# First products of the second stage with 128 rows, one chunk at a time

## The chip, the cores and the metric

One core of one Trainium2 chip runs the whole program. The metric is the device time of one execution in microseconds (us). The engines are TensorE (PE; its loads of weights are listed apart as PEld), VectorE (DVE), ScalarE (ACT), GpSimd (POOL) and SyncE (SP), which issues the transfers.

## What is computed

Windowed attention gives 2304 tokens of 512 numbers. A mixture of experts with 32 slots follows, and then a dense layer with 2048 hidden units, which is where the change lies. The reference, cut to these two:

```
def _moe_ref(x, phi, w1, w2):
    logits = x @ phi                              # 2304 x 32
    d = softmax of logits over the tokens
    slot_input = (d.T @ x).reshape(8, 4, 512)
    for e in range(8):
        slot_out[e] = np.maximum(slot_input[e] @ w1[e], 0.0) @ w2[e]
    c = softmax of logits over the slots
    return c @ slot_out                           # 2304 x 512

def _moe2_ref(x, w_in, w_out):
    h = x @ w_in                                  # 2304 x 2048
    g = h - np.tanh(h)
    return g @ w_out
```

Since the dense layer's input is `c @ slot_out`, its first product is `c @ (slot_out @ w_in)`: with `G = slot_out @ w_in` (32 x 2048) each hidden value needs a sum over 32 slots only.

## The kernel before, in words

The program runs through attention, the dispatch to the experts, the experts (`sop`, line 920), and from about 180 us the second stage, the function `second`. That stage treats the 2048 hidden units in 16 chunks `f` of 128, and the 18 blocks of 128 tokens in groups: A (blocks 0 to 3), EG (16 and 17), BG (4 to 7), C and DG (four blocks each). Its phases are, in order: A and EG with chunks 0 to 7, whose sums are put aside; BG with all 16 chunks; A and EG with chunks 8 to 15; C; DG.

For each batch of up to three chunks a projection comes first: `p` (line 1057) multiplies `slot_out` with four quarters of `w_in` into the four groups of 32 rows, `g` (line 1061) is its copy by ACT, and line 1065 multiplies that by the 128x128 matrix `dev` (in the tile `more`), which sums the four quarters and leaves the result in all four groups of 32 rows. ACT casts it to the tile `Gs` (line 1073); line 1067 makes `GT`, from which DVE gets the coefficients `co` (lines 1080 to 1083). `cT` holds the combine weights `c`, with tokens as columns, as four groups of 32 rows: high part, low part, high part, low part. A sum over 64 rows, high and low, is therefore the whole product.

A first product `h` (line 1191) takes a chunk's 128 columns of `Gs` as weights and streams the columns of `cT` of a group of tokens, 512 or, for EG, 256. `Gs` holds even chunks in rows 0 to 63 and odd ones in rows 64 to 127, and two chunks' products are issued one after the other, each on its own half of the rows by `tile_position`. Only the products of chunks 0 and 1 in the first phase are issued alone, each behind two products (line 1188) whose result is overwritten. From each `h` ACT makes `u` (line 1199), DVE makes `r` (line 1206), or for some chunks ACT makes `d` (line 1210) and POOL `r` (line 1214). Then, for each block of tokens, PE adds `r` times `wh`, the chunk of `w_out`, into `acc` (line 1163); one further product per block takes `cT` and `Ms`. `msum` and `mrep` make `Ms`. Weights come as 64-bit words in pieces `raw_i` and `raw_o`, from which POOL and ACT make halves (lines 348 to 353) that DVE merges (line 358). A later second load of all pieces (line 974, lines 979 and 981), `kmax`, `marks` and `verdict` check the ranges.

The order of all this is written by a planner, the class `Plan`: it is given each operation's engine, duration, inputs and buffers, lists the operations greedily by priority, tries 500 changes of the priorities, keeps the list with the least estimated end, and emits it. Each engine then works strictly in that order. Buffers that matter here: four PSUM tiles for `h` (shared with `p` and a few others), four for `acc`, three `u`, five `r`.

Of the kernel before, what the change touches and what calls it, by code (L numbers as in the profile page):

```python
# [11 lines left out]
F32R = mybir.dt.float32r  # L12
# [13 lines left out]
DM, NS, E, FE, FF = 512, 32, 8, 1024, 2048  # L26
# [57 lines left out]
class Plan:  # L84
# [4 lines left out]
    def add(self, *alts, deps=(), take=(), free=(), ready=0.0, boost=0.0):  # L89
        t = dict(alts=alts, deps=[d for d in deps if d is not None], take=take, free=free, ready=ready, boost=boost, id=len(self.tasks))  # L90
        self.tasks.append(t)
        for tag, key in take:
            if tag in self.ordered:
                self.ordered[tag].append(key)
        return t
# [178 lines left out]
def attention_moe_moe(ctx: ExitStack, tc: tile.TileContext, q, k, v, phi, w1, w2, w_in, w_out, cst, out, dbg=None):  # L274
    nc = tc.nc
# [680 lines left out]
    def second(raw, cT, store, more, wh0):  # L956
# [28 lines left out]
        DMA_AT = -0.5  # L985
        dev, devT, big = more[:, 0:128], more[:, 128:161], more[:, 161:].bitcast(F16)
        nc.vector.tensor_scalar(out=dev, in0=sel4, scalar1=sel4[:, NS - 1:NS], scalar2=0.125, op0=ALU.subtract, op1=ALU.mult)
        nc.vector.tensor_scalar(out=devT[:, 0:NS], in0=sel, scalar1=sel[:, NS - 1:NS], scalar2=5.0, op0=ALU.subtract, op1=ALU.mult)
        nc.gpsimd.memset(devT[:, NS:], 1.0 / NS)
        nc.gpsimd.memset(big, 2.0 ** 13)  # L990
        for f in range(NF // 2):
            nc.gpsimd.tensor_scalar(out=wh0[:, f, :], in0=place(("o", f)), scalar1=8.0, scalar2=0.0, op0=ALU.mult, op1=ALU.add)
        res, el, ps = yield
        Gs = res.tile([128, FF // 2], F32R, name="Gs")
        wh1 = res.tile([128, NF // 2, DM], F32R, name="wh1")
        whi = lambda f: (wh0 if f < NF // 2 else wh1)[:, f % (NF // 2), :]
        GT = res.tile([128, NF, NS + 1], F32, name="GT")
# [6 lines left out]
        live = {}  # L1004
        plan = Plan(dict(raw=RAW, h=4, acc=4, u=3, r=5, d=2, g1=2, o=8, code=2))
        add = plan.add

        def one(eng, dur, emit):
            return [(eng, dur, emit)]

        P = {}
# [3 lines left out]
        for k, piece in enumerate(PRE + loads):  # L1015
            kind, f = piece
# [27 lines left out]
            b = next(b for b in batches if f in b)  # L1044
            if f != b[-1]:
                continue
            n, f0 = len(b), b[0]
            tag = "acc" if f0 < 2 else "h"
            key = (tag, f0 if f0 < 2 else ("p", f0))
            def mk(b=b, n=n, f0=f0, tag=tag):  # L1050
# [15 lines left out]
                    for x in range(n):  # L1066
                        nc.tensor.matmul(t[:, 128 * n + 33 * x:128 * n + 33 * (x + 1)], lhsT=g1[:, 128 * x:128 * (x + 1)], rhs=devT, start=True, stop=True)

                def gs(y):
                    first = f0 + (f0 % 2 != y)  # L1070
                    m = len([x for x in b if x % 2 == y])
                    src = live["p", f0][64 * y:64 * y + 64, 0:128 * n].rearrange("p (n x) -> p n x", n=n)[:, first - f0::2]
                    nc.scalar.copy(Gs[64 * y:64 * y + 64, 128 * (first // 2):128 * (first // 2 + m)].rearrange("p (n x) -> p n x", n=m), src)

                def gt_copy():
                    nc.scalar.copy(GT[:, f0:f0 + n, :], live["p", f0][:, 128 * n:161 * n].rearrange("p (n x) -> p n x", n=n))
# [9 lines left out]
            fa, fg, fb, fh, ft, fc = mk()  # L1086
            lead = 8.0 - 2.0 * f0 if f0 < 2 else 0.0
# [2 lines left out]
                P["A", x] = a  # L1090
            g = add(one("ACT", 0.15 + 0.11 * n, fg), deps=[a], take=[("g1", f0)], boost=lead)
            bb = add(one("PE", 0.1 + 0.35 * n, fb), deps=[g], free=[("g1", f0)], boost=lead)
            for y in range(2):
                m = len([x for x in b if x % 2 == y])
                if m:
                    gh = add(one("ACT", 0.15 + 0.11 * m, lambda fh=fh, y=y: fh(y)), deps=[bb], free=[key], boost=lead)
                    for x in b:
                        if x % 2 == y:
                            P["G", x] = gh
            gc = add(one("ACT", 0.25, ft), deps=[bb], free=[key], boost=lead)  # L1100
            joint = next(y for y in joints if f0 in y)
            if f == joint[-1]:
# [31 lines left out]
        m = add(one("PE", 3.8, m_sum), deps=[P["pt", f] for f in range(NF)] + [P["mg", ("o", f)] for f in range(NF)], take=[("h", "m")])  # L1134
        m = add(one("ACT", 0.49, lambda: nc.scalar.activation(out=M4s, in_=live["m"], func=AF.Copy, scale=-2.0 / 15.0)), deps=[m], free=[("h", "m")])
        m = add(one("PE", 0.95, m_rep), deps=[m], take=[("h", "mr")])
        m = add(one("ACT", 0.49, lambda: nc.scalar.copy(Ms, live["mr"])), deps=[m], free=[("h", "mr")])
# [13 lines left out]
        for tiles, fs, aff, into in phases:  # L1151
# [20 lines left out]
            if aff == "first":  # L1172
                for t in tiles:
                    affine(t, phase_no)
            twos = [[f] for f in (0, 1)] if phase_no == 0 else []
            twos += [[f, f + 1] for f in fs if f % 2 == 0 and (phase_no or f > 1)]
            for two in twos:
                sub = tiles
                w, c0 = 128 * len(sub), 128 * sub[0]
                size = w / 512  # L1180
                idle = 2 if len(two) == 1 else 0
                name = lambda f, p=phase_no, t=tiles[0]: (p, f, t)

                def hid(two=two, w=w, c0=c0, name=name, idle=idle):
                    for f in two:
                        live["h", name(f)] = ps.tile([128, 512], F32, tag="h", name=f"h_{name(f)[0]}_{f}_{c0}", bufs=4)[:, 0:w]
                    for _ in range(idle):
                        nc.tensor.matmul(live["h", name(two[0])], lhsT=cT[:, 0:128], rhs=cT[:, c0:c0 + w], start=True, stop=True)
                    for f in two:
                        y = 64 * (f % 2)  # L1190
                        nc.tensor.matmul(live["h", name(f)], lhsT=Gs[y:y + 64, 128 * (f // 2):128 * (f // 2 + 1)], rhs=cT[y:y + 64, c0:c0 + w], start=True, stop=True, tile_position=(y, 0))  # L1191

                prev_h = h = add(one("PE", 0.03 + 0.23 * size + 0.35 * idle, hid), deps=[P["G", f] for f in two] + [prev_h], take=[("h", name(f)) for f in two])
                for f in two:
                    key = name(f)

# [348 lines left out]
```

## Time and profile before

| | |
|---|---|
| three runs | 299.88, 302.53, 305.98 us; median 302.53 |
| profiled execution | 302.16 us |
| its span | 300.3 us |
| busy, share of the span | PE 95%, DVE 67%, POOL 54%, ACT 50% |
| mean granted TensorE clock | 0.995 of full speed |
| `h` products (line 1191) | 80, 19.1 us busy |
| output products (`acc`, line 1163, without `Ms`) | 288, 80.3 us busy |

The span is from the first to the last instruction; the device time holds 1.9 us more around it. Matmuls are pipelined: a record's duration overlaps those of its neighbours, so the price of a product is read from the starts. A row of the timeline merges consecutive instructions of a kind: start, length, engine, line, what, how many.

### The profile page before, as it was taken

The numbers are of one execution on the slowest core, as the hardware profiler recorded it, in microseconds if no ns is written. First come the engines' busy times: TensorE is split into PE (matmuls) and PEld (weight loads), VectorE is DVE, ScalarE is ACT, GpSimd is POOL, SyncE is SP. The second block draws the span as 40 slices with busy tenths as digits, with TensorE's granted clock in tenths as the row PEclk, the third lists the DMA queues.
The fourth block names the chain that finished last, engine by engine and source line by source line (L and its number), as shares of the span: only waits on it lengthen the run. The fifth ranks groups of instructions, "written<-read, shape, count | busy, mean of one in ns | idle before, by whom it ended". The sixth has DMA issues, their size and how long they took to land.

```text
span 300.3 us, 7499 instructions
## 1 busy us (share of the span) xinstructions
PE 285.3 (95%) x2684; PEld 187.0 (62%) x2684; DVE 202.1 (67%) x693; ACT 151.4 (50%) x290; POOL 162.0 (54%) x240
## 2 busy tenths in 40 slices
PE   5999999999999999989999879999999999999991
PEld 3778888878788887653334215565665666576660
DVE  5559999688799897515323109889962768638972
ACT  2266655635374455421222018678863747757741
POOL 8639867865877660010516019981573657676320
PEclk9999999999999999999999999999999999999997
DMA  7989999879797889999999999952989999703004
GB/s 200 246 248 356 283 321 364 285 247 308 236 359 226 309 286 386 410 408 406 410 404 410 410 392 395 411 193 76 313 293 363 314 375 339 310 0 106 36 0 150
DMA packets 62699, 86.95 MB, mean 290 GB/s; under 512 B 19008, under 2 KB 48064, under 8 KB 62656
## 3 DMA queue, kind: packets, MB, share of 16 engines
q1 hardware_dynamic: 61568, 86.15, 82.4%
q8 instruction: 23, 0.38, 0.5%
q10 hardware_dynamic: 1088, 0.26, 0.4%
q14 instruction: 20, 0.16, 0.2%
HBM read 81.67 MB, written 4.72 MB: 288 GB/s over the span
## 4 chain that ended last, share of the span: by engine, by line
PE 78%; DMA 11%; DVE 5%; ACT 2%; issue 1%; SPq 0%; DVEq 0%; ACTq 0%
PE acc L1163 26%; PE sc L544 10%; PE pv L574 7%; PE pp L563 6%; PE h L1191 5%; DMA X<-in_moe_w 3%; DMA w<-in_moe_w 3%; DMA store<-in_moe_w 3%; PE tr_q L472 3%; PE xt L489 3%; PE tr_k L472 3%; PE sop L920 2%; PE lp L505 2%; PE hp L901 2%; PE sp L808 2%; PE warm L684 1%
## 5 line engine op out<-in xcount | busy, mean ns | idle before, releaser
L1163 PE MATMUL acc<-wh,r 128*128 128x512 f32 x288 | 80.3, 410 | 0.4 <-DVE r L1206 0.4
L1163 PEld LDWEIGHTS acc<-wh,r 128*128 128x128 f32 x288 | 50.7, 188 | 19.1 <-issue 7.0
L1199 ACT ACTIVATE u<-h,co 128x512 f32<-128x512 f32 (+1 forms) x80 | 48.8, 646 | 24.1 <-PE h L1191 17.1
L1206 DVE SCALAR_TENSOR_TENSOR r<-h,co,u 128x512 fp32r<-128x512 f32 (+1 forms) x66 | 43.8, 689 | 12.9 <-PE acc L1163 6.9
L548 DVE CUSTOM_DVE_ANT_0 sm<-sc,m_sb 128x96 f32<-128x96 f32 x144 | 29.2, 257 | 9.0 <-PE sc L544 9.0
L544 PE MATMUL sc<-kT,qT 64*64 64x96 f32 (+1 forms) x608 | 34.4, 253 | 0.3 <-ACT kT L465 0.3
L564 ACT ACTIVATE pT<-pp 96x512 f32<-96x512 f32 x38 | 23.1, 608 | 16.9 <-PE pp L563 16.9
L544 PEld LDWEIGHTS sc<-kT,qT 64*64 64x64 f32 x608 | 27.0, 134 | 5.0 <-issue 1.7
L1214 POOL TENSOR_TENSOR r<-d,u 128x512 fp32r<-128x512 f32 (+1 forms) x14 | 18.6, 1328 | 19.6 <-ACT d L1210 8.7
L439 POOL TENSOR_SCALAR vw<-vw 32x256 f32<-32x256 f32 (+1 forms) x40 | 24.9, 623 | 4.0 <-DMA vw<-in_v 1.1
L574 PE MATMUL pv<-vw,pT 97*64 97x65 f32 x608 | 26.1, 227 | 0.1
L482 ACT COPY qT<-tr_q 128x512 f32<-128x512 f32 x16 | 13.7, 858 | 24.6 <-PE tr_q L472 24.6
L574 PEld LDWEIGHTS pv<-vw,pT 97*64 97x64 f32 x608 | 20.8, 137 | 7.7 <-issue 6.5
L552 DVE TENSOR_TENSOR sm<-sm,mx 128x384 f32<-128x384 f32 (+1 forms) x38 | 24.7, 650 | 1.2
L563 PE MATMUL pp<-c_sb,sm 128*96 128x128 f32 x152 | 23.5, 277 | 0.1
L498 ACT COPY xT<-xt 128x512 f32<-128x512 f32 (+1 forms) x19 | 14.1, 767 | 11.0 <-PE xt L489 10.4
L1191 PE MATMUL h<-cT,Gs 64*128 64x512 f32 (+1 forms) x80 | 19.1, 468 | 0.0
L353 POOL TENSOR_SCALAR pre<-raw_o 128x512 bf16<-128x512 int16 x16 | 13.8, 870 | 9.3 <-DMA raw_o<-in_moe_w_out 8.9
L563 PEld LDWEIGHTS pp<-c_sb,sm 128*96 128x96 f32 x152 | 16.2, 126 | 3.2 <-issue 1.4
L606 DVE TENSOR_TENSOR X<-pv,rd 128x256 f32<-128x256 f32 (+3 forms) x52 | 16.5, 340 | 1.0
L901 PE MATMUL hp<-w,store 128*32 128x512 f32 x120 | 16.0, 596 | 1.2 <-DVE store L1386 1.2
L1191 PEld LDWEIGHTS h<-cT,Gs 64*128 64x128 f32 x80 | 7.5, 183 | 14.4 <-issue 9.8
(218 smaller groups left out, 479.0 us busy)
## 6 DMA issues: line engine op xcount, KB each, us to landing
w<-in_moe_w SPq DMA_DIRECT2D x54, 512.0 KB, 10.1
raw_i<-in_moe_w_in SPq DMA_DIRECT2D x32, 512.0 KB, 7.1
raw_o<-in_moe_w_out SPq DMA_DIRECT2D x32, 512.0 KB, 6.6
q<-in_q SPq DMA_DIRECT2D x16, 256.0 KB, 4.4
k<-in_k SPq DMA_DIRECT2D x16, 256.0 KB, 4.4
X<-in_moe_w SPq DMA_DIRECT2D x8, 512.0 KB, 9.4
out<-X SPq DMA_DIRECT2D x14, 256.0 KB, 3.8
vw<-in_v SPq DMA_DIRECT2D x16, 144.0 KB, 4.7
```

The source lines that it names most:

```text
L439: copy = lambda dst, src: nc.gpsimd.tensor_scalar(out=dst, in0=src, scalar1=1.0, scalar2=0.0, op0=ALU.mult, op1=ALU.add)
L544: nc.tensor.matmul(dst[half, lo:hi], lhsT=qT[u % NQ][half, i:i + QB], rhs=keys[half], start=True, stop=True)
L548: nc.vector.tensor_tensor_reduce(out=sm[:, o:o + n, :].rearrange("p g k -> p (g k)"), in0=sc[:, o:o + n, :].rearrange("p g k -> p (g k)"), ...
L552: nc.vector.tensor_tensor(out=sm[:, o:o + n], in0=sm[:, o:o + n], in1=mx[:, o:o + n].unsqueeze(2).to_broadcast([128, n, KB]), op=ALU.subtract)
L563: nc.tensor.transpose(pp[:, i, :], sm[:, i, :], ident)
L564: nc.scalar.activation(out=pT[0:KB], in_=pp, func=AF.Exp, scale=0.125)
L574: nc.tensor.matmul(pv[64 * ab:64 * ab + 64, i, :], lhsT=pT[:, o + x, 64 * ab:64 * ab + 64], rhs=w[:, ab, u % 2, j + x, :], start=x == 0, s ...
L901: nc.tensor.matmul(hp[32 * dc:32 * dc + 32, :], lhsT=siTs[e % 2][:, dc, :], rhs=w_of(f"1{e}", dc)[:, 512 * hf:512 * (hf + 1)], start=e % 2 ...
L1163: nc.tensor.matmul(live[key], lhsT=lhsT(), rhs=rhs(), start=new, stop=n == due)
L1191: nc.tensor.matmul(live["h", name(f)], lhsT=Gs[y:y + 64, 128 * (f // 2):128 * (f // 2 + 1)], rhs=cT[y:y + 64, c0:c0 + w], start=True, stop ...
L1199: nc.scalar.activation(out=live["u", key], in_=live["h", key], func=AF.Square, scale=co[:, SC, f:f + 1])
L1206: nc.vector.scalar_tensor_tensor(out=live["r", key], in0=live["h", key], scalar=co[:, BB, f:f + 1], in1=live["u", key], op0=ALU.add, op1=A ...
```

## The change

`Gs` gets a column range for every chunk (2048 columns instead of 1024). The right half of `dev` is set to zero by POOL, so that line 1065's product has zeros in rows 64 to 127; the cast to `Gs` takes all 128 rows and all chunks of a batch in one instruction. An `h` is one product over 128 rows, without a tile position: the first 64 rows give the sum over high and low part, the other 64 add zero. Each `h` is an operation of its own for the planner, with a new duration (0.004 + 0.228 for 512 columns, in place of 0.03 + 0.23 for a pair).

```diff
--- before.py
+++ after.py
@@ -985,13 +985,14 @@
         DMA_AT = -0.5
         dev, devT, big = more[:, 0:128], more[:, 128:161], more[:, 161:].bitcast(F16)
         nc.vector.tensor_scalar(out=dev, in0=sel4, scalar1=sel4[:, NS - 1:NS], scalar2=0.125, op0=ALU.subtract, op1=ALU.mult)
+        nc.gpsimd.memset(dev[:, 64:], 0.0)
         nc.vector.tensor_scalar(out=devT[:, 0:NS], in0=sel, scalar1=sel[:, NS - 1:NS], scalar2=5.0, op0=ALU.subtract, op1=ALU.mult)
         nc.gpsimd.memset(devT[:, NS:], 1.0 / NS)
         nc.gpsimd.memset(big, 2.0 ** 13)
         for f in range(NF // 2):
             nc.gpsimd.tensor_scalar(out=wh0[:, f, :], in0=place(("o", f)), scalar1=8.0, scalar2=0.0, op0=ALU.mult, op1=ALU.add)
         res, el, ps = yield
-        Gs = res.tile([128, FF // 2], F32R, name="Gs")
+        Gs = res.tile([128, FF], F32R, name="Gs")
         wh1 = res.tile([128, NF // 2, DM], F32R, name="wh1")
         whi = lambda f: (wh0 if f < NF // 2 else wh1)[:, f % (NF // 2), :]
         GT = res.tile([128, NF, NS + 1], F32, name="GT")
@@ -1066,11 +1067,8 @@
                     for x in range(n):
                         nc.tensor.matmul(t[:, 128 * n + 33 * x:128 * n + 33 * (x + 1)], lhsT=g1[:, 128 * x:128 * (x + 1)], rhs=devT, start=True, stop=True)
 
-                def gs(y):
-                    first = f0 + (f0 % 2 != y)
-                    m = len([x for x in b if x % 2 == y])
-                    src = live["p", f0][64 * y:64 * y + 64, 0:128 * n].rearrange("p (n x) -> p n x", n=n)[:, first - f0::2]
-                    nc.scalar.copy(Gs[64 * y:64 * y + 64, 128 * (first // 2):128 * (first // 2 + m)].rearrange("p (n x) -> p n x", n=m), src)
+                def gs():
+                    nc.scalar.copy(Gs[:, 128 * f0:128 * (f0 + n)], live["p", f0][:, 0:128 * n])
 
                 def gt_copy():
                     nc.scalar.copy(GT[:, f0:f0 + n, :], live["p", f0][:, 128 * n:161 * n].rearrange("p (n x) -> p n x", n=n))
@@ -1090,13 +1088,9 @@
                 P["A", x] = a
             g = add(one("ACT", 0.15 + 0.11 * n, fg), deps=[a], take=[("g1", f0)], boost=lead)
             bb = add(one("PE", 0.1 + 0.35 * n, fb), deps=[g], free=[("g1", f0)], boost=lead)
-            for y in range(2):
-                m = len([x for x in b if x % 2 == y])
-                if m:
-                    gh = add(one("ACT", 0.15 + 0.11 * m, lambda fh=fh, y=y: fh(y)), deps=[bb], free=[key], boost=lead)
-                    for x in b:
-                        if x % 2 == y:
-                            P["G", x] = gh
+            gh = add(one("ACT", 0.15 + 0.11 * n, fh), deps=[bb], free=[key], boost=lead)
+            for x in b:
+                P["G", x] = gh
             gc = add(one("ACT", 0.25, ft), deps=[bb], free=[key], boost=lead)
             joint = next(y for y in joints if f0 in y)
             if f == joint[-1]:
@@ -1172,13 +1166,11 @@
             if aff == "first":
                 for t in tiles:
                     affine(t, phase_no)
-            twos = [[f] for f in (0, 1)] if phase_no == 0 else []
-            twos += [[f, f + 1] for f in fs if f % 2 == 0 and (phase_no or f > 1)]
-            for two in twos:
+            for two in [[f] for f in fs]:
                 sub = tiles
                 w, c0 = 128 * len(sub), 128 * sub[0]
                 size = w / 512
-                idle = 2 if len(two) == 1 else 0
+                idle = 2 if phase_no == 0 and two[0] < 2 else 0
                 name = lambda f, p=phase_no, t=tiles[0]: (p, f, t)
 
                 def hid(two=two, w=w, c0=c0, name=name, idle=idle):
@@ -1187,10 +1179,9 @@
                     for _ in range(idle):
                         nc.tensor.matmul(live["h", name(two[0])], lhsT=cT[:, 0:128], rhs=cT[:, c0:c0 + w], start=True, stop=True)
                     for f in two:
-                        y = 64 * (f % 2)
-                        nc.tensor.matmul(live["h", name(f)], lhsT=Gs[y:y + 64, 128 * (f // 2):128 * (f // 2 + 1)], rhs=cT[y:y + 64, c0:c0 + w], start=True, stop=True, tile_position=(y, 0))
-
-                prev_h = h = add(one("PE", 0.03 + 0.23 * size + 0.35 * idle, hid), deps=[P["G", f] for f in two] + [prev_h], take=[("h", name(f)) for f in two])
+                        nc.tensor.matmul(live["h", name(f)], lhsT=Gs[:, 128 * f:128 * (f + 1)], rhs=cT[:, c0:c0 + w], start=True, stop=True)
+
+                prev_h = h = add(one("PE", 0.004 + 0.228 * size + 0.35 * idle, hid), deps=[P["G", f] for f in two] + [prev_h], take=[("h", name(f)) for f in two])
                 for f in two:
                     key = name(f)
```

Names in the following rows: `h_0_1024` is chunk 0 for the tokens from 1024 on; `r_10_16` is chunk 10 for the group that begins with block 16; the last number of a name counts tiles.

PE, the passage from phase EG with chunks 8 to 15 to phase C, before:

```order
L1191 MATMUL h_0_1024_3588<-cT,Gs 128x512
L1191 MATMUL h_1_1024_3589<-cT,Gs 128x512
L1163 MATMUL acc_17_3568<-wh_2793,r_11_16_3566 128x512
L1163 MATMUL acc_17_3568<-wh_2793,r_12_16_3575 128x512
L1163 MATMUL acc_16_3557<-wh_2793,r_12_16_3575 128x512
L1163 MATMUL acc_16_3557<-wh_2793,r_13_16_3586 128x512
L1163 MATMUL acc_17_3568<-wh_2793,r_13_16_3586 128x512
L1163 MATMUL acc_2_3448<-Ms,cT 128x512
L1163 MATMUL acc_16_3557<-wh_2793,r_14_16_3601 128x512
L1163 MATMUL acc_17_3568<-wh_2793,r_14_16_3601 128x512
L1191 MATMUL h_2_1024_3616<-cT,Gs 128x512
L1191 MATMUL h_3_1024_3617<-cT,Gs 128x512
```

and now:

```order
L1182 MATMUL h_0_1024_3602<-cT,Gs 128x512
L1182 MATMUL h_1_1024_3608<-cT,Gs 128x512
L1157 MATMUL acc_16_3573<-wh_2794,r_10_16_3551 128x512
L1182 MATMUL h_2_1024_3613<-cT,Gs 128x512
L1157 MATMUL acc_17_3580<-wh_2794,r_11_16_3583 128x512
L1157 MATMUL acc_16_3573<-wh_2794,r_12_16_3590 128x512
L1157 MATMUL acc_17_3580<-wh_2794,r_12_16_3590 128x512
L1157 MATMUL acc_16_3573<-wh_2794,r_15_16_3617 128x512
L1182 MATMUL h_3_1024_3627<-cT,Gs 128x512
L1157 MATMUL acc_16_3573<-wh_2794,r_13_16_3598 128x512
L1182 MATMUL h_4_1024_3632<-cT,Gs 128x512
```

The products `h`, which stood in pairs with eight output products between them, are spread: five of them now stand in the place of four, one, five and one output products apart.

DVE at the start of the second stage, from the first `r` to the second, before (`co` is of chunks 2 to 4, line 358 merges a weight piece, `raw_i_2708` being a later one than `raw_i_2704`):

```order
L1206 SCALAR_TENSOR_TENSOR r_0_0_2891<-h_0_0_2853,co,u_0_0_2882 128x512
L358 SCALAR_TENSOR_TENSOR X_76<-raw_i_2704,X_76 128x512
L1080 TENSOR_SCALAR co<-GT 128x3
L1081 TENSOR_TENSOR co<-co 128x3
L1082 TENSOR_SCALAR co<-co 128x3
L1083 SCALAR_TENSOR_TENSOR co<-co 128x3
L358 SCALAR_TENSOR_TENSOR X_76<-raw_i_2708,X_76 128x512
L1206 SCALAR_TENSOR_TENSOR r_1_0_2928<-h_1_0_2867,co,u_1_0_2910 128x512
```

and now:

```order
L1197 SCALAR_TENSOR_TENSOR r_0_0_2884<-h_0_0_2857,co,u_0_0_2875 128x512
L1078 TENSOR_SCALAR co<-GT 128x3
L1079 TENSOR_TENSOR co<-co 128x3
L1080 TENSOR_SCALAR co<-co 128x3
L1081 SCALAR_TENSOR_TENSOR co<-co 128x3
L358 SCALAR_TENSOR_TENSOR X_76<-raw_i_2704,X_76 128x512
L1197 SCALAR_TENSOR_TENSOR r_1_0_2910<-h_1_0_2879,co,u_1_0_2900 128x512
```

The merge of `raw_i_2708` has moved behind the second `r`; the merge of `raw_o_2700`, which stood ahead of the first coefficients, has moved to a place far behind.

PE at the same place, from the second half of the projection of chunk 1 on, before (`h_0_0_2853<-cT` are the products that are overwritten, `p_2820` is the projection of chunks 2 to 4, `p_2843` of 5 to 7):

```order
L1067 MATMUL p_2813<-more,g_1_2831 128x33
L1057 MATMUL p_2843<-pre,phi_sb 32x384 x4
L1188 MATMUL h_0_0_2853<-cT 128x512 x2
L1191 MATMUL h_0_0_2853<-cT,Gs 128x512
L1188 MATMUL h_1_0_2867<-cT 128x512 x2
L1191 MATMUL h_1_0_2867<-cT,Gs 128x512
L1065 MATMUL p_2820<-g_2_2858,more 128x384
L1067 MATMUL p_2820<-more,g_2_2858 128x33 x3
L1065 MATMUL p_2843<-g_5_2865,more 128x384
L1067 MATMUL p_2843<-more,g_5_2865 128x33 x3
L1163 MATMUL acc_0_2897<-wh_2692,r_0_0_2891 128x512
```

and now:

```order
L1068 MATMUL p_2814<-more,g_1_2832 128x33
L1058 MATMUL p_2844<-pre,phi_sb 32x384 x4
L1180 MATMUL h_0_0_2857<-cT 128x512 x2
L1182 MATMUL h_0_0_2857<-cT,Gs 128x512
L1066 MATMUL p_2821<-g_2_2862,more 128x384
L1068 MATMUL p_2821<-more,g_2_2862 128x33 x3
L1180 MATMUL h_1_0_2879<-cT 128x512 x2
L1182 MATMUL h_1_0_2879<-cT,Gs 128x512
L1066 MATMUL p_2844<-g_5_2869,more 128x384
L1068 MATMUL p_2844<-more,g_5_2869 128x33 x3
L1182 MATMUL h_2_0_2902<-cT,Gs 128x512
```

A half of a projection now stands between the first two `h`, and a third `h` ahead of the first output product; the projection of chunks 8 to 10 (`p_2914` before) has moved from the first phase to the change from the second to the third.

POOL, where the second stage's constants are set, before (`more` holds `dev`, in its first 128 columns, and two smaller constants; `wh_2692` is `wh0`):

```order
L922 MEMSET store 128x8x4 x2
L922 MEMSET X_76 128x8x4 x2
L989 MEMSET more 128x1
L990 MEMSET more 128x32
L992 TENSOR_SCALAR wh_2692<-pre 128x512 x8
L353 TENSOR_SCALAR X_76<-raw_i_2696 128x512
```

and now:

```order
L922 MEMSET store 128x8x4 x2
L922 MEMSET X_76 128x8x4 x2
L988 MEMSET more 128x64
L990 MEMSET more 128x1
L991 MEMSET more 128x32
L993 TENSOR_SCALAR wh_2692<-pre 128x512 x8
L353 TENSOR_SCALAR X_76<-raw_i_2696 128x512
```

The memset of the right half of `dev` stands ahead of the two small ones and the eight copies of `wh0`.

## Rows read from the trace of the kernel before

**Rows 1.** Chain that ended last, 192.7 to 294 us: shares by line.
```profile
by line: PE acc L1163 75.7%; PE h L1191 14.8%; PE msum L1128 3.5%; PE p L1057 1.3%; PE p L1065 1.1%; PE p L1067 0.9%; PE mrep L1132 0.8%; DVE okt L1318 0.5%; DVE okt L1317 0.4%; PE marks L1341 0.3%; PE kmax L1274 0.2%; issue 0.2%; DVE okt L
```

**Rows 2.** Windows: us; busy of PE, PEld, DVE, ACT, POOL; clock; DMA share; GB/s.
```profile
180.00:205.00 25.00, 24.41 (x138) 14.54 (x130) 22.52 (x54) 18.63 (x43) 20.77 (x29) 1.00 0.80 303
192.70:206.70 14.00, 13.99 (x58) 8.61 (x58) 12.47 (x31) 9.82 (x20) 8.86 (x16) 1.00 0.52 187
206.70:224.70 18.00, 18.00 (x89) 11.48 (x89) 14.74 (x25) 14.07 (x28) 9.88 (x19) 1.00 0.78 264
224.70:294.00 69.30, 69.30 (x300) 43.93 (x299) 47.24 (x96) 42.23 (x73) 37.56 (x42) 1.00 0.59 207
```

**Rows 3.** Chain that ended last, 179.5 to 193 us, in order of time.
```profile
182.90 1.20 DVE pre L358
...
189.62 0.69 DVE X L358
```

**Rows 4.** PE in order of time, 264.5 to 290 us.
```profile
267.16 0.51 PE L1191 MATMUL h<-cT,Gs 64*128 64x512 f32 x2
267.60 3.91 PE L1163 MATMUL acc<-wh,r 128*128 128x512 f32 x16
271.43 0.50 PE L1191 MATMUL h<-cT,Gs 64*128 64x512 f32 x2
271.87 0.73 PE L1163 MATMUL acc<-wh,r 128*128 128x512 f32 x2
272.53 0.51 PE L1191 MATMUL h<-cT,Gs 64*128 64x512 f32 x2
```

**Rows 5.** PE in order of time, 196.4 to 203.5 us.
```profile
198.47 0.38 PE L1191 MATMUL h<-cT,Gs 64*128 64x256 f32 x2
198.78 1.18 PE L1163 MATMUL acc<-wh,r 128*128 128x512 f32 x4
199.89 0.38 PE L1191 MATMUL h<-cT,Gs 64*128 64x256 f32 x2
```

**Rows 6.** PE in order of time, 205 to 225 us.
```profile
206.78 0.85 PE L1057 MATMUL p<-X,phi_sb 128*32 128x384 f32 x8
207.57 0.73 PE L1163 MATMUL acc<-wh,r 128*128 128x512 f32 x2
...
209.69 0.81 PE L1065 MATMUL p<-g,more 128*128 128x384 f32 x2
210.34 0.75 PE L1067 MATMUL p<-more,g 128*128 128x33 f32 x6
210.92 2.35 PE L1163 MATMUL acc<-wh,r 128*128 128x512 f32 x9
213.20 0.73 PE L1191 MATMUL h<-cT,Gs 64*128 64x512 f32 x4
213.86 2.37 PE L1163 MATMUL acc<-wh,r 128*128 128x512 f32 x9
```

**Rows 7.** PE's groups by shape, 192.7 to 294 us.
```profile
L1191 PE MATMUL h<-cT,Gs 64*128 64x512 f32 x60 | 14.5, 490 | 0.0
...
L1191 PE MATMUL h<-cT,Gs 64*128 64x256 f32 x16 | 3.1, 381 | 0.0
```

**Rows 8.** PE in order of time, 273.4 to 277 us.
```profile
276.32 0.39 PE L1163 MATMUL acc<-Ms,cT 128*128 128x512 f32 x1
276.56 0.63 PE L1163 MATMUL acc<-wh,r 128*128 128x512 f32 x2
```

**Rows 9.** POOL in order of time, 150 to 180 us.
```profile
157.80 5.42 POOL L992 TENSOR_SCALAR wh<-pre 128x512 fp32r<-128x512 f32 x8
178.47 0.77 POOL L353 TENSOR_SCALAR X<-raw_i 128x512 bf16<-128x512 int16 x1 [15.25 <-DMA raw_i<-in_moe_w_in]
```

**Rows 10.** DVE in order of time, 160 to 171 us.
```profile
164.31 0.28 DVE L987 TENSOR_SCALAR more<-c_sb 128x128 f32<-128x128 f32 x1
```

**Rows 11.** Instructions on the tile h: duration ns min/median/max, first and last start.
```profile
L1199 ACT ACTIVATE u<-h,co x80: 467/688/712, 185.0 to 288.3; 128x512 f32<-128x512 f32 x64, 128x256 f32<-128x256 f32 x16
L1206 DVE SCALAR_TENSOR_TENSOR r<-h,co,u x66: 469/743/753, 186.7 to 289.6; 128x512 fp32r<-128x512 f32 x52, 128x256 fp32r<-128x256 f32 x14
```

## Prediction

> **What bounds the kernel now.** I read the chain that ended last first. From 192.7 us to the verdict near 294 us it runs on TensorE alone: 75.7% of that stretch are the output products (line 1163), 14.8% are the first products `h` (line 1191) that the change rewrites, some 15 us [rows 1]. The windows agree: PE is busy in every microsecond of the three stretches behind 192.7, at a granted clock of 1.00, while DVE and ACT have room, but little of it at first: DVE works 12.47 of 14.0 us, then 14.74 of 18.0, then 47.24 of 69.3 [rows 2]. So behind 192.7 a microsecond less on PE is a microsecond less of the kernel, as long as the other engines follow. Before 192.7 it is not: there the chain runs through DVE, over merges of the weights, coefficients and the first `r` [rows 3]. The end (verdict, flag, last store) hangs on the last PE products and moves with them; both programs have four output products behind the verdict.
>
> **What a visit to `h` costs on PE.** I take starts, since ends are modelled. Two visits with 16 output products between them start 4.27 us apart, two with 2 between them 1.10 us [rows 4]: 14 products make 3.17 us, 0.23 each, and 1.10 - 2 x 0.23 leaves 0.64 for the visit, a pair of 512 columns. Other such gaps give 0.62 to 0.64; I use 0.63. The two of a pair run side by side, or they could not be back within 0.44 us [rows 4]; a block of two pairs is back after 0.66, so the second pair adds about 0.23 and the block costs 0.86 [rows 6]. So 0.23 of a visit is streaming, and about 0.40 is paid for going to 64-row tiles and back. A pair of 256 columns: 1.42 us from one visit to the next with 4 products between [rows 5] leaves 0.50, its neighbours 0.51 and 0.53; I use 0.515.
>
> **What it will cost.** The new `h` is a product with 128 rows, 128 columns of weights and 512 or 256 streamed columns. The trace holds it under another name: `acc<-Ms,cT` has the same shape and type with `cT` as one operand, stands among output products, and the next starts 0.23 us later [rows 8]. I price an `h` of 512 columns at 0.23. One of 256 is not in the trace. Below it cannot be under the six 33-column records, 0.58 us together, 0.10 each [rows 6]; above, not over the 0.23 of 512. I take 0.12, half of 0.23, nearer to the lower end, because 0.10 at 33 columns shows that the exchange of weights does not hold it longer. Sixteen of them: 1.9, between 1.6 and 3.7.
>
> **The sum on the path.** Behind 192.7 stand 60 `h` of 512 columns and 16 of 256 [rows 7]: 26 single pairs and two blocks of four, and eight pairs of 256. Of the 26, 24 lie between output products: 24 x (0.63 - 0.46) = 4.1. Two follow work of another kind whose own change of kind stays, so I give them half, 0.2. The blocks of four lose: 2 x (0.86 - 0.92) = -0.1. The narrow pairs: 8 x (0.515 - 0.24) = 2.2. Together 6.3 us; with 256 columns at 0.23 it would be 4.5, at 0.10 6.7. Of the 6.3, the visits before 224.7 (five pairs, one behind the projection, both blocks of four, four narrow pairs) hold 1.9, the rest 4.4.
>
> **What moves, and what that costs.** The planner gets new durations, so all engines are re-ordered from chunk 0 on. At the start, DVE does two merges less before the third `r`, worth 1.20 + 0.69 us by the rows of two of them [rows 3]. But PE has not yet done the projection of chunks 8 to 10 when it goes on; a batch of that shape costs 0.79 (206.78 to 207.57) and 1.23 (209.69 to 210.92), 2.0 us [rows 6], and that now falls behind 192.7. The two nearly cancel; I take 0, with 1.9 earlier and 2.0 later as the ends. There is one more change between projection and other work there, also ahead of the path.
>
> The new memset stands on POOL in front of the eight copies of `wh0`, and waits for DVE's line 987, which runs at 164.31 [rows 10]. The copies ran from 157.80 for 5.42 us; after them POOL sat idle 15.25 us, until 178.47 [rows 9]. Now they go from about 164.6 to 170.1, 8 us before POOL is wanted. Nothing waits for them before the first output product, so the cost is nothing; if that cover were gone it would be up to 6.8 us. The memset itself is like the two small ones beside it. ACT has seven casts of `Gs` where it had twelve, each of all 128 rows and at most 384 columns; ACT works 18.63 of the 25 us from 180 to 205 [rows 2], so I count nothing. The larger `Gs` shifts the tiles behind it; the waits of the first instructions there name loads that end before the stage, so nothing either.
>
> **New waits.** An `h` needs one `u` (median 688 ns) and one `r` (743 ns) before its output products [rows 11]: with the steps between some 2.3 us, ten PE products. In the new order, counted at the prices above, a single `h`, a narrow one with shorter `u` and `r`, has less PE work than that between itself and its first use. What can fail is the rate. From 180 to 205 DVE works 22.52 of 25.0 us [rows 2]; it has 2.5 us to give, and PE will ask for 1.9 by 224.7. That fits, but not in every place, since DVE is strictly in order and its merges stand between the `r`. I take off 0.7, between 0 and the whole 1.9. Gain: 6.3 - 0.7 = 5.6. The profiled execution took 302.16 us, its span 300.3 and 1.9 around it, 0.4 under the median of the three runs: 302.16 - 5.6 = **296.6 us**.
>
> **Rivals.** First, *DVE and ACT become the bound until 224.7*: the 1.9 are lost, and about 1.0 more (one late `r` a phase, five phases, at the price of a product, 0.23) further on: gain 3.4, 298.8. For it: DVE at 89% and 90% early. Against it: 2.5 us idle, and room behind 224.7. Second, *all of it and the start too*: no new waits, and one merge less on DVE's chain ahead of 192.7 counts: 6.3 + 1.0 = 7.3, 294.9. Third, *the new order alone eats the gain*: PE meets unready operands at the changes of phase, six times about 1 us: 302. Fourth, slower: *the 0.40 is not the tiles'*, but is paid by any visit to `h`, for instance for its other bank or weights. Then the pairs, two for one, were the cheap form. The new order visits `h` 61 times instead of 39, some 58 of them on the path: 58 x 0.40 - 6.3 = 16.9 more, 319. It decides from 0.11 us a visit (6.3 / 58). Against it: `acc<-Ms,cT` also brings other weights and pays nothing [rows 8].
>
> The trace shows that the two of a pair share 0.23 us of streaming [rows 4, 6]. The Trainium skill ("TensorE: Matmul & The Clock Gate", the table under "Why this matters for your kernels") advises just that form for products with few rows: sliced into row groups they run concurrently, and a small one alone takes as long as a full one. By that rule alone, without the price of the change of tiles, splitting 30 pairs and 8 narrow ones would cost 30 x 0.23 + 8 x 0.12 = 7.9 us, 310; it is a milder form of the fourth rival and shares its chance. The same skill ("TensorEngine Tiling (Array Packing)", Key Properties) says that a change of the tiling mode drains the engine; the 0.40 us of a visit here agree.
>
> **How the numbers follow.** Forecast 296.6: 0.56, itself from 295.3 to 297.8. First rival 0.20, second 0.14, third 0.06, fourth 0.04. A change under 2%, about 6.0 us, can hardly be told from none here; 302.16 - 6.0 = 296.1 cuts the forecast's own range, and I put 0.24 of its 0.56 below it. Faster: 0.24 + 0.13 of the second = 0.37; slower: the fourth and a third of the third, 0.06; same: 0.57. The range takes in the first and second rival and about 1 us of spread between runs: 293.9 to 299.9.
>
> **What would show it.** In the new profile `h` has 128*128 rows; an `h` between output products starts 0.23 behind its forerunner and the next 0.23 behind it (0.12 if narrow); no step of 0.32 or 0.43 stays around it. POOL's copies of `wh0` start near 164.6. PE's waits for `r` total under 1.5 us. I am wrong if the step behind `h` is above 0.3, if a narrow `h` holds the next product 0.23, or if PE waits for DVE several microseconds between 193 and 225.

## The result

| | before | after |
|---|---|---|
| median of six runs, us | 302.92 (299.88 to 305.98) | 299.18 (297.79 to 300.20) |
| ratio, with its 95% interval | | 0.9887 (0.9846 to 0.9928) |
| profiled execution, its span | 302.16, 300.3 | 297.79, 296.0 |
| the stage | 113.80 | 110.21 |

The kernel is 1.1% faster: 3.7 us by the medians, where 5.6 were forecast. The ratio leaves out the run of 305.98, over 1.5% above the fastest of the kernel before. "The stage" is here the time from the start of the first `p` product to the start of the last output product, in the profiled execution. It gained 3.58 us. The profiled executions differ by 4.37, because this one also reached the first `p` 1.36 us earlier and took 0.63 longer behind the last output product. In the runs below the first `p` comes between 178.4 and 182.7 us, though they compute the same ahead of it but for the small memset; so the 1.36 is not the change's, and I compare stages. Part of that spread may be the clock's: in e1, e5, e7 and e8 the granted clock stood at 0.50 for 3.4 us between 134 and 141 us, long ahead of the stage.

Line 1182 is now `h`, 1157 the output product, 1197 `r`. First the chain that ended last behind 190.1 us, by lines, then two windows (columns as in [rows 2]).

```profile
by line: PE acc L1157 60.4%; PE h L1182 16.3%; PE msum L1122 3.6%; DVE r L1197 3.3%; PE p L1058 2.2%; PE p L1066 1.7%; PE p L1068 1.6%; DVE scw L1271 1.5%; DVE X L1253 1.3%; issue 1.2%; DVE store L981 1.1%; PE mrep L1126 0.9%; DVE scw L1272
```
```profile
190.06:221.40 31.34, 31.34 (x160) 23.07 (x164) 28.82 (x58) 24.73 (x48) 18.34 (x31) 1.00 0.74 255
221.40:288.70 67.30, 66.59 (x301) 49.31 (x300) 46.88 (x94) 41.47 (x72) 37.39 (x43) 1.00 0.60 213
```

In [rows 1] the chain was PE's alone but for the verdict. Now it leaves PE for DVE: for `r`, for the tests of the verdict (`scw`), for the sums with the parts put aside (line 1253) and the range check (line 981). By modelled ends PE is without work in the second window, for 0.71 us, and not in the first.

The prices of the products are the forecast ones. PE in order of time, around narrow and wide `h`:

```profile
193.79 0.28 PE L1182 MATMUL h<-cT,Gs 128*128 128x256 f32 x1
193.91 0.40 PE L1157 MATMUL acc<-wh,r 128*128 128x512 f32 x1
194.14 0.28 PE L1182 MATMUL h<-cT,Gs 128*128 128x256 f32 x1
...
266.91 0.40 PE L1182 MATMUL h<-cT,Gs 128*128 128x512 f32 x1
267.15 1.09 PE L1157 MATMUL acc<-wh,r 128*128 128x512 f32 x4
268.08 0.39 PE L1182 MATMUL h<-cT,Gs 128*128 128x512 f32 x1
268.31 0.63 PE L1157 MATMUL acc<-wh,r 128*128 128x512 f32 x2
```

A wide `h` holds the next product 0.23 us (268.08 to 268.31), a narrow one 0.12, and the step into an `h` is 0.23. The 0.44 and the 0.31 around the pairs of [rows 4, 5] are gone.

The rest is waits. PE is late five times, at 187.93, 190.06, 245.29, 252.49 and 281.23 us; three of these on PE, then the DVE and POOL work behind the late `r`:

```profile
187.93 0.70 PE L1157 MATMUL acc<-wh,r 128*128 128x512 f32 x2 [1.00 <-DVE r L1197]
188.47 0.86 PE L1182 MATMUL h<-cT,Gs 128*128 128x512 f32 x3
...
252.49 0.50 PE L1157 MATMUL acc<-wh,r 128*128 128x512 f32 x1 [0.45 <-DVE r L1197]
252.83 0.39 PE L1182 MATMUL h<-cT,Gs 128*128 128x512 f32 x1
...
281.23 0.50 PE L1182 MATMUL h<-cT,Gs 128*128 128x512 f32 x1 [0.16 <-DVE r L1197]
281.57 1.98 PE L1157 MATMUL acc<-wh,r 128*128 128x512 f32 x8
```
```profile
185.91 1.21 DVE L358 SCALAR_TENSOR_TENSOR X<-raw_i,X 128x512 int32<-128x512 int32 x1
187.05 0.74 DVE L1197 SCALAR_TENSOR_TENSOR r<-h,co,u 128x512 fp32r<-128x512 f32 x1
...
244.56 0.28 DVE L1216 TENSOR_REDUCE emx<-u 128x1 f32<-128x128 f32 x1 [0.74 <-ACT u L1190]
244.76 1.13 DVE L1197 SCALAR_TENSOR_TENSOR r<-h,co,u 128x256 fp32r<-128x256 f32 x2
...
250.00 1.78 DVE L981 SCALAR_TENSOR_TENSOR store<-store 128x512 int32<-128x512 int32 x1
251.70 2.05 DVE L1197 SCALAR_TENSOR_TENSOR r<-h,co,u 128x512 fp32r<-128x512 f32 x3
...
277.53 1.26 DVE L1271 TENSOR_TENSOR scw<-scw 128x16 f32<-128x16 f32 x1
```
```profile
249.94 1.29 POOL L1205 TENSOR_TENSOR r<-d,u 128x512 fp32r<-128x512 f32 x1
...
277.48 1.29 POOL L1205 TENSOR_TENSOR r<-d,u 128x512 fp32r<-128x512 f32 x1 [1.44 <-ACT d L1201]
```

Since ends are modelled, I count a wait as the step from an `h` or an output product to the next one less 0.23 (0.12 behind a narrow `h`), where that is over 0.15 us; steps that a change of tiles lengthens are left out. The one of 0.40 behind `mrep`, there in every kernel, is left out. The five waits are 1.16, 0.42, 0.26, 0.62 and 0.43 us, 2.89 together; the step that follows each is about 0.1 too long as well (252.49 to 252.83 is 0.34), 0.51 together. Before had one wait, 0.53, and 0.11 behind it. So 3.40 - 0.64 = 2.76 us of new waits, and 3.58 + 2.76 = 6.34 us of cheaper products.

That this is the 6.3 of the forecast is in part luck. The 6.34 are of the whole stage, the 6.3 of the path behind 192.7 alone. The count also has no place for two things. Before waited for ACT at 190.30, where the step was 0.72 and the like one at 184.61 is 0.43:

```profile
189.58 0.50 PE L1191 MATMUL h<-cT,Gs 64*128 64x512 f32 x2
190.30 0.91 PE L1065 MATMUL p<-g,more 128*128 128x384 f32 x2 [0.23 <-ACT g L1061]
```

And the kernel after has three more steps that are too long, ahead of 257.31, 261.94 and 272.78 us, each under the 0.15, which hold 0.6 us with the steps that follow them. The clean test of the price is e1, below.

### The profile page after: what moved, and what is told of

It reads as the page before. It is cut to its first block, busy times and chain, and to the rows that moved or that the text cites. A ratio compares the mean times of both kernels' runs of the same rounds, so it can differ in the third digit from the quotient of the medians.

```text
span 296.0 us, 7506 instructions
## 1 busy us (share of the span) xinstructions
PE 277.9 (94%) x2684; PEld 193.9 (66%) x2684; DVE 200.2 (68%) x695; ACT 150.6 (51%) x284; POOL 161.4 (55%) x240
## 4 chain that ended last, share of the span: by engine, by line
PE 58%; DMA 22%; DVE 10%; POOL 3%; issue 2%; SPq 2%; ACT 1%; POOLq 0%; DVEq 0%; ACTq 0%
PE acc L1157 20%; DMA w<-in_moe_w 10%; PE sc L544 7%; PE h L1182 5%; PE pv L574 5%; PE pp L563 4%; DMA raw_i<-in_moe_w_in 4%; DMA X<-in_moe_w 3%; PE xt L489 3%; PE tr_q L472 2%; DMA raw_o<-in_moe_w_out 2%; DVE r L1197 2%; PE tr_k L472 2%; PE lp L505 1%; PE msum L1122 1%
## 5 line engine op out<-in xcount | busy, mean ns | idle before, releaser
L1157 PE MATMUL acc<-wh,r 128*128 128x512 f32 x288 | 78.3, 397 | 1.5 <-DVE r L1197 1.4
L1157 PEld LDWEIGHTS acc<-wh,r 128*128 128x128 f32 x288 | 52.9, 188 | 15.5 <-DVE r L1197 1.7
L1190 ACT ACTIVATE u<-h,co 128x512 f32<-128x512 f32 (+1 forms) x80 | 49.7, 648 | 21.9 <-PE h L1182 10.7
L1182 PE MATMUL h<-cT,Gs 128*128 128x512 f32 (+1 forms) x80 | 28.6, 393 | 0.4 <-DVE r L1197 0.4
L552 DVE TENSOR_TENSOR sm<-sm,mx 128x384 f32<-128x384 f32 (+1 forms) x38 | 24.1, 635 | 1.2
L1182 PEld LDWEIGHTS h<-cT,Gs 128*128 128x128 f32 x80 | 14.8, 188 | 7.7 <-DVE r L1197 2.1
```

Source lines behind the costliest of these rows:

```text
L552: nc.vector.tensor_tensor(out=sm[:, o:o + n], in0=sm[:, o:o + n], in1=mx[:, o:o + n].unsqueeze(2).to_broadcast([128, n, KB]), op=ALU.subtract)
L1157: nc.tensor.matmul(live[key], lhsT=lhsT(), rhs=rhs(), start=new, stop=n == due)
L1182: nc.tensor.matmul(live["h", name(f)], lhsT=Gs[:, 128 * f:128 * (f + 1)], rhs=cT[:, c0:c0 + w], start=True, stop=True)
L1190: nc.scalar.activation(out=live["u", key], in_=live["h", key], func=AF.Square, scale=co[:, SC, f:f + 1])
```

## The experiments

All times in us; waits as counted above, without the steps that follow them. So the wait for the first `r`, behind a projection, is not in them (but for e5, where it is the only one): by idle time it is 0.56 in e1 and e6, 0.17 in e9, 0.48 in e10, 0.45 in e11 and 0.70 in e12. "Low price" is what the planner of the kernel before reckoned for a pair, or half of it for a single product; "true" is what the rows show.

| kernel | stage | waits | device time |
|---|---|---|---|
| before | 113.80 | 0.53 | 302.92 |
| after (singles, true price) | 110.21 | 2.89 | 299.18 |
| e1, pairs, low price | 108.42 | 1.26 | 297.12 (6 runs) |
| e2, after, merges later | 110.40 | 3.03 | 299.00 (6 runs) |
| e3, after, less side work | 108.46 | 1.70 | 297.04 (1) |
| e4, after, 64-row products | 128.88 | 0 | 317.03 (1) |
| e5, pairs, true price | 112.00 | 2.5, then half clock | 299.79 (4 runs) |
| e6, e1 with another draw | 109.28 | 2.00 | 298.15 (1) |
| e7, after with another draw | 109.04 | 1.65 | 301.41 (1) |
| e8, after, more DVE work | 110.63 | 3.47 | 301.59 (1) |
| e9, e10, e5 with other draws | 110.90, 111.29 | 3.46, 2.88 | 300.88, 299.58 (1 each) |
| e11, e12, singles, low price, two draws | 112.03, 112.06 | 4.51, 3.59 | 300.91, 300.45 (1 each) |

**e1: the new product in the old order.** Before's pairs, casts by parity and planner prices, with `Gs` at full width:

```diff
-   nc.scalar.copy(Gs[64 * y:64 * y + 64, ...], src)       # src: 64 rows
+   nc.scalar.copy(Gs.rearrange("p (n x) -> p n x", n=NF)[:, first:f0 + n:2], src)   # 128 rows
-   nc.tensor.matmul(..., lhsT=Gs[y:y + 64, ...], rhs=cT[y:y + 64, c0:c0 + w], ..., tile_position=(y, 0))
+   nc.tensor.matmul(..., lhsT=Gs[:, 128 * f:128 * (f + 1)], rhs=cT[:, c0:c0 + w], ...)
+   nc.gpsimd.memset(dev[:, 64:], 0.0)
```

> The order of the kernel before, instruction for instruction on PE, DVE, ACT and SP (the first products in pairs, the planner's old durations), with the 128-row products of the kernel after. First theory, a matter of the order: the product itself saves 6.3 us of PE's path wherever it stands, and what the kernel after lost to waits for r (2.8 us more than before) came with its new order. Then this kernel has hardly a new wait, the stage from the first projection to the start of the last output product is 107.5 to 108.5 us long (113.8 before, 110.2 after), and the time is 5 to 6 us under the kernel before, ratio 0.980 to 0.984. Second theory, a matter of rate: DVE can't follow a PE that is 6 us faster, in whatever order. Then the waits are here too, 2 to 3 us of them, the stage is about 110 us and the ratio 0.987 to 0.990. Third, the order of single products is itself the gain: ratio 0.995 to 1.0.

Ratio 0.9804 (0.9747 to 0.9860), stage 108.42: the first theory, though not without new waits. PE in order of time, two pairs with 16 output products between, the place that answers to [rows 4]:

```profile
264.32 0.63 PE L1191 MATMUL h<-cT,Gs 128*128 128x512 f32 x2
264.79 3.79 PE L1164 MATMUL acc<-wh,r 128*128 128x512 f32 x16
268.42 0.63 PE L1191 MATMUL h<-cT,Gs 128*128 128x512 f32 x2
```

4.10 us from visit to visit where [rows 4] have 4.27: 0.17 a pair, the forecast's own term. Since PE does the same in the same order as before, the path itself can be compared, from the output product that waits last at the start to the last one of the stage:

```profile
192.71 1.19 PE L1163 MATMUL acc<-wh,r 128*128 128x512 f32 x4 [0.36 <-DVE r L1206]
```
```profile
189.25 1.17 PE L1164 MATMUL acc<-wh,r 128*128 128x512 f32 x4 [0.56 <-DVE r L1206]
...
194.31 1.20 PE L1164 MATMUL acc<-wh,r 128*128 128x512 f32 x4 [0.40 <-DVE r L1206]
```

From 192.71 it is 100.93 us before, from 194.31 it is 95.58 here: 5.35 less. Behind there e1 has waits of 0.30 and 0.39, with their following steps 0.92, and before has none, so the cheaper products save 6.27 us on the path: the forecast's 6.3, shown. Ahead of it nothing is gained, 12.83 us against 12.87: there DVE sets the time, and what PE saves it spends waiting (0.72 us at 189.25, by the step). So DVE follows a PE that is 6.3 us faster with a loss of 0.9 on the path; that the kernel after is 1.8 us slower than this one comes with its order, the only other difference being how ACT's casts are cut.

**e2: merges behind the `r`.**

```diff
+   for f, behind in ((10, 2), (11, 4), (12, 6)):   # merge of raw_i f goes behind r of chunk `behind`
+       m = todo.pop(...); todo.insert(... + 1, m)
```

> The kernel after, with DVE's merges of the pieces raw_i of chunks 10, 11 and 12 moved behind r of chunks 2, 4 and 6 of the first phase; everything else in the same order. First theory: PE waits at 187.93 (1.16 us) and 190.06 (0.42 us) because these merges, 1.2 us each beside POOL's copies, stand in DVE's queue ahead of an r whose u has long been there. Then both waits go, the stage is 108.5 to 109.0 us instead of 110.2, and the projections of chunks 8 to 13 are not late. Rival: the sum of DVE's work ahead of the steady part is what counts, and a later merge only moves the wait: the stage stays within 0.4 us of 110.2, with waits of the same total a few us later, or at the projections.

The rival was right. The waits at the start only move and come to 1.71 (1.58 after); PE now meets them at the narrow `h`:

```profile
194.22 0.39 PE L1187 MATMUL h<-cT,Gs 128*128 128x256 f32 x1 [0.36 <-DVE r L1202]
...
196.66 0.39 PE L1187 MATMUL h<-cT,Gs 128*128 128x256 f32 x1 [0.77 <-DVE r L1202]
```

**e8: more work for DVE at the start.** One copy of 128x512 behind the merge for chunk 10.

```diff
+   if piece == ("i", 10):
+       nc.vector.tensor_copy(wh1[:, 7, :], place(("o", 0)))
```

> The kernel after with one more operation on DVE, a copy of 128x512 behind the merge for chunk 10 and ahead of the first r; its result is overwritten later, the order of all else is the same. If DVE's sum of work sets the time until PE runs steadily (as the merges moved without gain in e2 say), PE's waits there grow by the copy's whole duration, 0.6 to 0.8 us, and the stage is 110.8 to 111.1 us. If DVE has slack there and the waits are those of one place, they grow by less than 0.3 us.

Between the two: the copy held DVE 0.92 us (187.83 to 188.75), the waits at the start grew from 1.58 to 2.17 and the stage by 0.42, half of the copy.

```profile
187.83 1.00 DVE L1000 CAST wh<-pre 128x512 fp32r<-128x512 f32 x1
188.75 0.73 DVE L1201 SCALAR_TENSOR_TENSOR r<-h,co,u 128x512 fp32r<-128x512 f32 x1
```
```profile
192.44 0.70 PE L1161 MATMUL acc<-wh,r 128*128 128x512 f32 x2 [1.64 <-DVE co L1082]
```

With e2: at the start the sum of DVE's work counts more than which of it stands in front, but half of the added work was taken up.

**e3: less side work on DVE.** Leaves out the look at all but four pieces of the second load and the tests of the coefficients.

```diff
-   nc.vector.scalar_tensor_tensor(out=seen, in0=t, ...)      # line 981
+   pass
+   if part < 2:
+       nc.vector.memset(ok[:, 2 * part:2 * part + 1 + (part == 0)], 1.0 - part)
+   return                                                     # judge_b
```

> The kernel after, leaving out part of the range check: of the second load only the first four pieces are looked at, and DVE's tests of the coefficients ahead of the verdict are replaced by constants; the order of all else is the same. First theory: the waits at 252.49 (0.62 us) and 281.23 (0.43 us) stand behind this side work in DVE's queue, so both are gone, and the wait at 245.29 (0.26 us) stays or shrinks, since what stands ahead of it is ACT's u; the stage is 109.0 to 109.4 us instead of 110.2. Rival: these waits are the planner's own edges (r in the order just where PE wants it), and come again in the same places: 110.0 or more.

The three late waits are gone, that of 245.29 too but for 0.04, and the stage is 1.76 shorter, more than the 0.8 to 1.2 expected. The waits of PE, from the first `p` on (in us, times, longest):

```profile
PE acc L1157 <- DVE r L1197: 1.1, 1, 1.1
PE p L1058 <- ACT phi_sb L938: 0.4, 1, 0.4
PE h L1182 <- DVE r L1197: 0.3, 1, 0.3
```

Only those of the start (189 and 191 us) are left. That the late waits come from side work is shown for all of it together; which of the two kinds makes which wait is read only from the rows above. At 245.29 none of what was left out stands right ahead of the `r`: there it is a short reduction (`emx`) that waits for ACT's `u`.

**e4: 64 rows, one at a time.**

```diff
-   lhsT=Gs[:, 128 * f:128 * (f + 1)], rhs=cT[:, c0:c0 + w], ...
+   lhsT=Gs[0:64, 128 * f:128 * (f + 1)], rhs=cT[0:64, c0:c0 + w], ..., tile_position=(0, 0)
```

> The kernel after, each first product over 64 rows alone (the lower half of Gs and cT, tile position 0); the order is the same. If the 0.40 us that a visit costs is the change to 64-row tiles and back, each visit between 128-row products pays it, pair or not: about 60 visits, 24 us less the waits that it covers, some 320 us, with steps of 0.43 and 0.32 around each h. If it was the two products on different rows together, or their crossing each other, a single 64-row product costs the 0.23 of a 128-row one and the time stays at about 298 us.

The change of tiles it is. Same order, PE in order of time:

```profile
188.97 0.96 PE L1182 MATMUL h<-cT,Gs 64*128 64x512 f32 x3
189.87 0.74 PE L1157 MATMUL acc<-wh,r 128*128 128x512 f32 x2
...
283.40 0.49 PE L1182 MATMUL h<-cT,Gs 64*128 64x512 f32 x1
283.82 1.20 PE L1157 MATMUL acc<-wh,r 128*128 128x512 f32 x4
284.94 0.49 PE L1182 MATMUL h<-cT,Gs 64*128 64x512 f32 x1
```

From 283.40 to 284.94 are 1.54 us with four output products between; 1.54 - 4 x 0.23 leaves 0.62, what a pair costs in [rows 4]. Three 64-row products in a row hold PE 0.90 us (188.97 to 189.87), so the second and third cost 0.23 each: it is the change that is paid for, not the 64 rows. Over the stage: 18.67 longer than after, and the 3.40 of waits covered, 22.1 for 61 visits, 0.36 each. The Trainium skill ("TensorEngine Tiling (Array Packing)", Key Properties) says that a change of the tiling mode drains the engine; the runs agree, with these 0.36 us a visit.

**e5, e6, e7, e9 to e12: the draw and the prices.** The planner's search gets another start of its random numbers (3, 5 or 9 for 2), or another price of `h`.

```diff
-   prev_h = h = add(one("PE", 0.03 + 0.23 * size + 0.35 * idle, hid), ...)                  # pairs, low price
+   prev_h = h = add(one("PE", (0.004 + 0.228 * size) * len(two) + 0.35 * idle, hid), ...)   # pairs, true price
-   prev_h = h = add(one("PE", 0.004 + 0.228 * size + 0.35 * idle, hid), ...)                # singles, true price
+   prev_h = h = add(one("PE", 0.015 + 0.115 * size + 0.35 * idle, hid), ...)                # singles, low price
```

> Full-width first products issued in pairs, as in e1, but the planner is told what they take (0.464 for two of 512 columns, 0.236 for two of 256) where it counted 0.26 and 0.145 in e1; so the whole order is new. Theory of the prices: the order of e1 had few waits because it was made for a PE faster than the real one, so each r stands earlier than PE needs it; with true prices the r come just in time and waits of 2 to 3 us are back: stage 109.8 to 111 us (108.4 in e1, 110.2 after), ratio to before 0.985 to 0.992. Theory of the pairs: two products at a time put DVE and ACT ahead by one r, and this remains: stage 108.0 to 109.0, ratio 0.980 to 0.983.

> The kernel e1 with another start of the planner's random numbers: the same prices, the same pairs, another order. If prices or pairs give the small waits, the stage is again 108.0 to 109.0 us. If the order of e1 was one lucky draw, the stage is 109.4 to 111 us, with waits in other places.

> The kernel after with another start of the planner's random numbers; nothing else. If waits of 2.9 us belong to the form (single products, true prices), the stage is 109.9 to 110.9 us, with 2.3 to 3.5 us of waits in other places. If they are one unlucky draw, the stage is 108.0 to 109.3 us.

> Pairs at the full width with the true prices, as e5, with the random numbers of e6 (109.28 us in the stage at the low prices). If low prices make the better order, this is over 109.8 us; if draws differ by chance alone, it lies anywhere between 108.4 and 110.5, as likely under e6 as over it. The stage of e5, 112.0 us, had 2.5 us of one wait and 2.6 us of half clock behind it; without such a wait it can't be over 111.

> As e9, with a third start of the random numbers. Low prices better: over 109.8 us, and the mean of the three draws with true prices over that of the two with low ones (108.85) by 1 us or more. Chance alone: 108.4 to 110.5.

> The kernel after (single products) with the planner's price of a first product halved, 0.015 + 0.115 for 512 columns, that is half of what the kernel before counted for two. If low prices make the better order, the stage is 108.5 to 109.4 us instead of 110.2, with under 2 us of waits. If not, 109.5 to 111.

> As e11, with the random numbers of e7 (109.04 us at the true price). If low prices make the better order, under 108.7 us; if chance alone, 108.4 to 110.5.

e5 was worse than either theory had it, since a wait of 2.5 us took the clock with it (below). Its profiled execution was the slowest of four, 300.85 us where the others took 298.00 to 300.33, and 2.8 us of the 112.00 are that clock's. e6 fell between the two; e7 was the better of two draws for its form. Pairs give 108.42 and 109.28 at the low price and 112.00, 110.90 and 111.29 at the true one, in the mean 108.85 against 111.40 (110.5 without the 2.8): for these few the theory of low prices holds. Singles turn it round: 110.21 and 109.04 at the true price, 112.03 and 112.06 at the low one (e11, e12). So it falls as a rule. What stands is the spread: with the same products the order alone moves the stage by 3.6 us, from 108.4 to 112.1, and no rule for a good one came out of these nine draws.

## Why the prediction came out as it did

- **The time**: the median, 299.18, lies in the stated range but above the forecast's own 295.3 to 297.8. That the profiled execution, 297.79, just reaches it is luck: 1.36 us of its 4.37 came ahead of the stage. With the order kept (e1) the stage gains 5.4 us and the medians 5.8, which is what was forecast.
- **The bound** (PE behind 192.7): right. Cheaper products shorten the stage until PE waits for DVE, and in e1 save nothing ahead of that point (12.83 against 12.87).
- **The price of a visit, 6.3 us on the path**: right, 6.27 by e1. The four terms as they stand make 6.4, not 6.3, a slip within the rounding. The 0.23 and 0.12, the blocks of four that gain nothing, the 0.40 of the tiles: all as the rows said. The fourth rival falls with e4: a single 64-row product pays, a 128-row one doesn't.
- **The start, 0**: the waits there with their following steps are 1.77, before's were 0.64 (0.93 with that for ACT), so they cost 1.13 (0.84), inside the ends of -2.0 and 1.9. DVE's sum of work has much to do with it (e2, e8); I had let two merges less and a projection later cancel, and set no price on a PE that gets there before DVE.
- **The new waits, 0.7**: this is the term that was mis-sized. Forecast were 0.7; counted are 1.63 behind the start, 2.2 with the three small ones, and not where I looked. I watched DVE's rate until 224.7; between 190.4 and 245 there is no new wait. They came at 245 to 281, where [rows 2] show DVE with a third of its time free, at 252.49 and 281.23 because one `r` stood in the strict order behind side work that can wait; without the side work all three go, but for 0.04 us (e3). The first rival named the right sum, 2.9 lost, and time, 298.8, but by a rate in the first phases and a few tenths at each change of phase, which isn't what happened.
- **The sum**: 6.34 - 1.13 - 1.63 = 3.58 against 5.6 forecast. It comes out by its making, since the 6.34 were got from the 3.58 and the waits, and shows only where the loss lies. The tail, counted at nothing, took 0.63 more in this execution; in the orders of the table it lies between 6.7 and 8.1 us, and I didn't follow it.
- **The memset**: right. POOL's copies moved by 5.8 us and still end 8 us before POOL is wanted; answers to [rows 9]:

```profile
163.26 0.18 POOL L988 MEMSET more<- 128x64 f32 x1 [7.02 <-DVE more L987]
...
163.59 5.50 POOL L993 TENSOR_SCALAR wh<-pre 128x512 fp32r<-128x512 f32 x8
177.09 0.77 POOL L353 TENSOR_SCALAR X<-raw_i 128x512 bf16<-128x512 int16 x1 [8.00 <-DMA raw_i<-in_moe_w_in]
```

- **Waits under 1.5 us** as a sign: wrong, 2.89 by starts (the view of waits, by modelled ends, has 1.8).

Best of the kernels that do all the work is e1, 2.0% under the kernel before (1.4 to 2.5%): the new product, in the old order. What is open: why its order is better than most draws.

## What to carry to other kernels

Here a product over half the rows is dearer than a padded one when it stands alone between full-height products, and a pair of them dearer than two padded ones; count the steps into and out of it before packing. Where a planner or a search makes the order, an edit to one duration redraws all of it: run the edit in the old order first, and two or three draws of the new, before crediting or blaming the edit. Low average use of an engine says nothing about one late operand: look at what non-urgent work stands ahead of it in the strict order. And where the order is kept, compare the same instruction in both traces, rather than adding up waits.

## Unexpected of the hardware

- **A wait of 2.5 us on PE cost as much again.** In e5 PE waited 2.52 us for an `r`. The granted clock, 1.00 before, averaged 0.69 in the stretch of the wait and then stood at 0.50, the lower of the two levels (1.2 GHz against 2.4), until about 199.8. Windows, and PE there:

```profile
190.00:192.00 2.00, 1.34 (x9) 0.96 (x7) 1.90 (x8) 0.09 (x1) 1.94 (x3) 1.00 1.05 424
192.00:194.40 2.40, 0.55 (x1) 0.50 (x2) 2.40 (x6) 2.28 (x6) 2.16 (x7) 0.69 1.03 415
194.40:196.00 1.60, 1.60 (x5) 1.26 (x4) 1.53 (x7) 0.14 (x1) 0.48 (x2) 0.50 1.01 415
196.00:199.80 3.80, 3.80 (x10) 2.93 (x10) 1.95 (x4) 2.11 (x4) 3.02 (x5) 0.51 1.05 405
199.80:203.00 3.20, 3.20 (x17) 2.66 (x17) 2.39 (x6) 2.04 (x5) 3.08 (x5) 1.00 0.51 207
```
```profile
193.85 2.93 PE L1164 MATMUL acc<-wh,r 128*128 128x512 f32 x6 [2.52 <-DVE r L1206]
```

  Twelve steps there are 0.427 instead of 0.23, and with the two at the edges 2.8 us are lost. The waits of 1.16 (after) and 1.80 us (e8) were followed by no such steps.
- **A 16-column DVE operation took 1.26 us** (277.53, above) where its neighbours take 0.17: it began 0.05 us behind POOL's two-operand `r` and ended with it. The check at 250.00 took 1.78 beside the other POOL `r`, and 0.67 with none beside it at 253.68. Where the check came first, at 258.17, it was POOL's `r`, 0.04 us behind it, that took longer, 1.80 instead of 1.29. The Trainium skill ("SBUF — State Buffer", Terms) says that DVE and GpSimd share a port pair, exclusively for a whole instruction; the rows agree, in either order. `r` on DVE, which reads PSUM, kept its 0.74 or 0.75 beside every `r` of POOL.

```profile
253.68 0.67 DVE L981 SCALAR_TENSOR_TENSOR store<-store 128x512 int32<-128x512 int32 x1
...
258.17 0.69 DVE L981 SCALAR_TENSOR_TENSOR store<-store 128x512 int32<-128x512 int32 x1 [1.11 <-POOL store L974]
```
```profile
258.21 1.80 POOL L1205 TENSOR_TENSOR r<-d,u 128x512 fp32r<-128x512 f32 x1
```

- **Each wait costs 0.1 more than itself**: at full clock the step that follows it is 0.31 to 0.34 instead of 0.23 (0.22 instead of 0.12 behind a narrow `h`), in every kernel above that waits.
